# The second layer of six token groups computed with two levels of a seven-product scheme, and four engines put in a fixed order

## The chip, the core and the metric

One core of a Trainium2 chip runs the whole program. It has a matrix engine (PE; PEld is its weight load), a vector engine (DVE), an activation engine (ACT), a GpSimd engine (POOL) and a sync engine (SP) whose queue issues nearly all DMAs. The metric is the device time of one execution in microseconds (us); the time shown is the median of three runs.

## The reference, cut to what matters

The input has 8 batches of 576 tokens, 8 heads of 64, so a model width of 512. Attention with two softmaxes (over the features of q, over the tokens of k) gives x; a Fourier mix and a two-layer network follow.

```python
q_s = softmax(q, axis=-1); k_s = softmax(k, axis=2)          # both written out with max, exp, sum
kv = einsum('bhsd,bhse->bhde', k_s, v)
x = einsum('bhsd,bhde->bhse', q_s, kv)                       # then (B, S, H*D)
u = x + real(fft(fft(x, axis=1), axis=2))
un = (u - mean(u)) / sqrt(var(u) + 1e-06)
out = u + max(un @ w_ch1, 0.0) @ w_ch2                       # w_ch1: 512 x 2048, w_ch2: 2048 x 512
```

## The kernel before, in words

All is in 32-bit floating point. The 4608 tokens are cut into nine groups of 512: one for each batch (group number `g` below 8), and a shared one (`g` equal to `B`) with the tokens that the folding of the Fourier transform treats apart. They are worked on in the order 0 to 6, shared, 7; `order` or `at` counts the place in that order, 0 to 8. Place 0 is computed plainly while the weights are converted and combined. For places 1 to 8 both layers use one level of a scheme that multiplies two 2 x 2 block matrices with seven block products instead of eight. The sums of weight blocks are made once and lie in DRAM (`w1s`, `w2s`).

- **First layer**, `up` (line 945). For each of four `j` there are seven products of 256 x 256 x 256 for each of two hidden pairs, in the order `ORDER` (line 77). `strassen` (line 906) keeps three PSUM banks. Product 1 goes to `ba`, 6 to `bb`, 5 to `bc`; 7 adds onto `bb`, 2 onto `ba`, 4 onto `bb`, 3 onto `bc`. Between them the banks are read: ACT copies `ba` to `s1` (line 921), DVE makes `u2` and `u3` from `bb` (lines 925, 929), `other` adds and ACT applies the relu (lines 968, 969), and POOL makes four sums of hidden blocks (`a_side`, lines 362 to 365).
- **Second layer**, `down` (line 982). Seven products, each 2 halves of tokens times 8 pairs of hidden blocks, so 16 matmuls of 128 x 128 weights with 256 columns (line 995). DVE adds the results to x (line 1020); POOL adds three of the intermediate sums (line 1007).
- **Weights.** The combined weights are fetched again for each place: `load` (line 410) brings chunk `n`, 15 for a place (8 of `w1s`, 7 of `w2s`), into one of four 1 MiB places of `big`. `used` (line 978) releases a chunk after its last matmul and so issues the load of chunk `n + 4`.
- **Work beside it.** While place `order` is computed, the attention of batch `order + 1` runs beside the first layer (`attention`, line 430: keys `k_load`, `k_exp`, `k_turn`, `k_times_v`; queries `q_load`, `q_exp`, `q_turn`, `q_times_kv`; for even batches also a tail item `t`, with `t_turn` and `t_fold`), and the mix (`transform` line 686, `mix_own`, `mix_shared`) and the normalisation of the next group (`norm`, line 816) beside the second.

The order: `merged` (line 93) deals the side steps evenly among the main steps, and the planner of the framework then orders each engine's instructions by priority and its own cost estimates, and sets the semaphores. Each engine runs its instructions in the order it was given. `gate` (line 489) is a tiny DVE instruction that makes a DMA target wait.

Of the kernel before, what the change touches and what calls it, by code (L numbers as in the profile page):

```python
# [40 lines left out]
F32 = mybir.dt.float32  # L41
I32, U32 = mybir.dt.int32, mybir.dt.uint32
ACT = mybir.ActivationFunctionType
ALU = mybir.AluOpType
# [32 lines left out]
ORDER = (1, 6, 5, 7, 2, 4, 3)  # L77

# [45 lines left out]
class _Block:  # L124
    def __init__(self, ctx, tc, q, kT, v, w1, w2, ft, cd, out):
# [42 lines left out]
        self.w2s = d.tile([7, P, NP, HD], F32, tag="w2s", name="w2s", bufs=1)  # L168

# [239 lines left out]

    def load(self, n):  # L410

        g, i = divmod(n, NP + 7)
        if g > B:
            return
        k = n % 4
        w = self.big[:, k * NP * HD:(k + 1) * NP * HD].rearrange("p (a n) -> p a n", n=HD)
        if i < NP:
            self.nc.sync.dma_start(w[:, 0:7, :], self.w1s[i][:])
        else:
            self.nc.sync.dma_start(w, self.w2s[WB_AT[ORDER[i - NP]]])  # L420
        self.stream[n] = w

    def hpairs(self, p, n):

        a = 2 * NF * D + p * 7 * HD if p < NP // 2 else NF * D + (p - NP // 2) * 7 * HD
        return self.big[:, a:a + n * 7 * HD].rearrange("p (a s n) -> p a s n", s=7, n=HD)
# [3 lines left out]
    def attention(self, b, loads=None):  # L430


        items = [("k", b, r) for r in range(NR)]
        tail = [("t", b)] if b % 2 == 0 else []
        own = [("q", b, c, u) for c in range(2) for u in range(2)]

        if b == 1:
            items = []
        items = items + tail + own if b else items[:2] + tail + items[2:] + own
        kinds = {"k": (self.k_load, self.k_exp, self.k_turn, self.k_times_v),  # L440
                 "q": (self.q_load, self.q_exp, self.q_turn, self.q_times_kv),
                 "t": (self.t_load, self.q_exp, self.t_turn, self.t_fold)}
        stage = lambda i: (lambda it: kinds[it[0]][i](it))
        load, *stages = [stage(i) for i in range(4)]
        if loads is None:
            stages.insert(0, load)
        else:
            loads += [lambda it=it: load(it) for it in items]
        steps = pipelined(items, stages)

        steps.insert(len(steps) if b else 8, lambda: self.t_times_kv(b))
        return steps
# [45 lines left out]
    def k_load(self, it):  # L498
        nc, (_, b, r) = self.nc, it
        if b == 0:  # L500
            ks, v = self.at_start[:2]
            self.live[it] = [ks[r], v[:, :, r * P:(r + 1) * P]]
            return
        if b == 1:
            self.live[it] = [self.second_at[0][:, r * S:(r + 1) * S], self.second_at[1][r]]
            return
        if r > 1:
            self.keys_to(b, r, *self.key_places())

    def keys_to(self, b, r, k, v):  # L510
        nc = self.nc
        nc.sync.dma_start(k, self.kT[b, r * P:(r + 1) * P, :])
        cols = slice(r * P, (r + 1) * P)
        nc.sync.dma_start(v[:, 0:4, :], self.v[b, 0:512, cols].rearrange("(c p) n -> p c n", p=P))
        nc.sync.dma_start(v[:, 4, :], self.v[b, S - P:, cols])
        self.live["k", b, r] = [k, v]
# [5 lines left out]
    def keys_from(self, b, t):  # L522


        for r in range(2):
            k, v = self.key_places()
            self.keys_to(b, r, k, v)
            self.gate(t, k[0:1, 0:1])
# [9 lines left out]
    def k_exp(self, it):  # L538
        nc, V = self.nc, self.nc.vector
        k = self.live[it][0]  # L540
        m = self.small.tile([P, 1], F32, tag="km", name="km", bufs=3)
        V.reduce_max(m[:], k, axis=AX.X, negate=True)
        rec = self.small.tile([P, 1], F32, tag="krec", name="krec", bufs=3)
        nc.scalar.activation(k, k, ACT.Exp, bias=m[:, 0:1], accum_out=rec[:, 0:1])
        V.tensor_scalar(out=rec[:], in0=rec[:], scalar1=ATT_EPS, scalar2=None, op0=ALU.add)
        V.reciprocal(rec[:], rec[:])
        self.live[it].append(rec)
# [15 lines left out]
    def k_times_v(self, it):  # L563
# [3 lines left out]
        for c in range(NC):  # L567
            nc.tensor.matmul(pk, lhsT=ks[:, c, :], rhs=v[:, c, :], start=(c == 0), stop=(c == NC - 1))  # L568
        for h in range(2):
# [29 lines left out]
    def q_exp(self, it):  # L599
        nc, V = self.nc, self.nc.vector  # L600
        q = self.live[it][0]
        heads = q.rearrange("p (h d) -> p h d", h=H)
        spread = lambda t: t[:].unsqueeze(2).to_broadcast([P, H, DH])
        m = self.small.tile([P, H], F32, tag="qm", name="qm", bufs=3)
        V.reduce_max(m[:], heads, axis=AX.X, negate=True)  # L605
        for h in range(H):
            nc.scalar.activation(heads[:, h, :], heads[:, h, :], ACT.Exp, bias=m[:, h:h + 1])  # L607
        rec = self.small.tile([P, H], F32, tag="qrec", name="qrec", bufs=4)
# [3 lines left out]
        if it[:2] == ("q", 0) and it[2] == it[3]:  # L612


            self.live[it].append(spread(rec))
            return
# [21 lines left out]
    def t_fold(self, it):  # L638
# [4 lines left out]
        for e, op, i in ((G, ALU.add, 0), (V, ALU.subtract, 2)):  # L643
            e.tensor_tensor(out=T[:, :, i, 1:NT], in0=q[:, :, 1:NT], in1=q[:, :, W - 1:W - NT:-1], op=op)
            e.tensor_tensor(out=T[:, :, 1 + i, 1:NT - 1], in0=q[:, :, Q - 1:Q - NT + 1:-1],
                            in1=q[:, :, Q + 1:Q + NT - 1], op=op)
        n = NT - 1
# [5 lines left out]
    def q_times_kv(self, it):  # L653
# [3 lines left out]
        for r in range(NR):  # L657
            nc.tensor.matmul(px[:, r * P:(r + 1) * P], lhsT=qT[:, r, :], rhs=self.kvr[b % 2][:, r, :], start=True,  # L658
                             stop=True)
        x = self.xpart(b, c, u)  # L660
# [6 lines left out]
    def t_times_kv(self, b):  # L667
# [9 lines left out]
        nc.scalar.copy(self.xshared(b // 2)[part], px[W:])  # L677
        V.scalar_tensor_tensor(out=g[:, 1:HD], in0=g[:, D - 1:HD:-1], scalar=self.sign[:, 0:1], in1=g[:, 1:HD],
# [3 lines left out]
        self.live["g", b] = g  # L682
# [3 lines left out]
    def transform(self, b):  # L686
# [36 lines left out]
        def folded():  # L723
            columns_again()
# [39 lines left out]

        folds = [tokens_folded, columns_folded, by_frequency, folded] if b else [at_first]
# [140 lines left out]
    def strassen(self, product, out, early=lambda *a: None):  # L906
# [30 lines left out]
        for m in ORDER:  # L937
# [4 lines left out]
            steps.append(begin + parts + end)  # L942
        return steps

    def up(self, at, unT):

        nc, V = self.nc, self.nc.vector
        steps = []
        for j in range(NP // 2):
            pairs = (2 * j, 2 * j + 1)  # L950
            hp = lambda i, h=self.hpairs(2 * j, 2): h[:, :, i, :]

            def product(m, bank, first, last, pairs=pairs):
                def run(i):
                    w = self.stream[15 * at + pairs[i]]
# [19 lines left out]
            steps.append([s for m in job for s in m] + [lambda p=p: self.used(15 * at + p) for p in pairs])  # L975
# [6 lines left out]
    def down(self, g, at):  # L982
        nc, V = self.nc, self.nc.vector
        h = [self.hpairs(p, 1)[:, 0] for p in range(NP)]
        last = at == B

        def product(m, bank, first, final):
            n = 15 * at + NP + ORDER.index(m)
# [3 lines left out]
            def run(i, q):  # L992
                w = self.stream[n]
                for p in range(4 * q, 4 * q + 4):
# [36 lines left out]
        return [s for m in steps for s in m]  # L1031
# [22 lines left out]
def kernel(ctx: ExitStack, tc: tile.TileContext, q, kT, v, w1, w2, ft,  # L1054
# [56 lines left out]

    groups = [*range(B - 1), B, B - 1]
    for order, g in enumerate(groups):
        loads = [] if g == 0 else None
        one, two = front(order + 1, loads) if order + 1 < B else (blk.later, [])
        if g == 0:
# [16 lines left out]
            combine[NP:NP] = [lambda i=i: blk.load(15 + i) for i in range(3)]  # L1133
            combine.append(lambda: blk.load(18))
# [26 lines left out]
        jobs, down = blk.up(order, nexts.pop(g)), blk.down(g, order)  # L1161
# [57 lines left out]
```

## Time and profile before

| what | value |
|---|---|
| median of three runs | 1124.38 us (1123.99 to 1129.22) |
| the profiled execution's own time | 1128.05 us |
| its span, first to last instruction | 1126.2 us |
| mean granted TensorE clock | 0.991 |
| PE busy | 1088.4 us (97%) |
| DVE, ACT, POOL busy | 545.4, 403.5, 331.9 us |
| DMA | 193.79 MB, mean 172 GB/s |

A matmul of 32-bit numbers shows as two PE instructions ("passes") in the trace, each with its weight load. A pass's listed duration (379 ns for 256 columns) includes the time in which the next one has already begun, so the cost of a pass is the distance to the next: the chain of waits merges neighbouring passes, and its "us" over its "xcount" is that distance. In the lines of groups the columns are: source line, engine, operation, out<-in, shapes, count, then busy us and mean ns, then the engine's idle time before them with what ended it. In the timeline they are start, duration, engine, line, operation. The page's slices and the stretches ("windows") give busy us of each engine, the granted clock, the DMA engines' mean busy share and GB/s.

### The profile page before, as it was taken

Reading aid. Unit: us, or ns where it says so; the run is one execution under the profiler, and the core shown is the slowest. Engines: PE = TensorE matmul, PEld = TensorE weight load, DVE = VectorE, ACT = ScalarE, POOL = GpSimd, SP = SyncE. Lnnn points to the kernel's source line nnn. Section 1 sums busy time; section 2 is a strip of 40 time slices with the busy share of each in tenths; the row PEclk is TensorE's granted clock in tenths of the full one; section 3 lists DMA queues with packets and bytes.
Section 4 is the critical chain, followed back from the end, with each engine's and each line's share of the span. In section 5 each row is a group of like instructions: output and inputs, shape, how many; then the busy total and the mean of one; then the engine's idle time right before and its main releaser. Section 6 shows DMA issues by size and latency. Waiting matters only on the chain.

```text
span 1126.2 us, 14461 instructions
## 1 busy us (share of the span) xinstructions
PE 1088.4 (97%) x5376; PEld 909.9 (81%) x5376; DVE 545.4 (48%) x1121; ACT 403.5 (36%) x973; POOL 331.9 (29%) x303
## 2 busy tenths in 40 slices
PE   5789989999999999999999999999999999999997
PEld 4644545887888888898889888888889888888886
DVE  6694796368423734375344643583444352103301
ACT  6695434255233513362325332542334152201200
POOL 1065571235013510324024402251034203402320
PEclk8899999999999999999999999999999999999999
DMA  9555786464246534554356435642453444434451
GB/s 305 176 190 188 259 291 220 145 224 166 98 150 211 195 127 145 195 172 171 125 173 221 150 106 190 198 185 108 147 191 150 144 144 144 187 141 157 152 187 56
DMA packets 92581, 193.79 MB, mean 172 GB/s; under 512 B 23120, under 2 KB 59728, under 8 KB 85344
## 3 DMA queue, kind: packets, MB, share of 16 engines
q1 hardware_dynamic: 90712, 191.82, 49.9%
q10 hardware_dynamic: 1800, 1.05, 0.3%
q8 instruction: 43, 0.70, 0.2%
q14 instruction: 26, 0.21, 0.1%
HBM read 168.72 MB, written 28.31 MB: 175 GB/s over the span
## 4 chain that ended last, share of the span: by engine, by line
PE 81%; POOL 3%; issue 2%; ACT 1%; DVE 1%; ACTq 0%; POOLq 0%
PE bb L957 14%; PE bb L995 14%; PE bc L995 10%; PE ba L957 9%; PE bc L957 9%; PE ba L995 9%; PE acc L568 2%; PE acc L658 2%; PE bc L896 2%; PE acc L752 1%; PE acc L776 1%; PE acc L755 1%; PE tr L857 1%; PE tr L554 1%; PE tr L623 1%
## 5 line engine op out<-in xcount | busy, mean ns | idle before, releaser
L957 PE MATMUL bb<-unT,big 128*128 128x256 f32 x768 | 187.4, 381 | 0.2 <-DVE u L925 0.2
L995 PE MATMUL bb<-big 128*128 128x256 f32 x768 | 172.1, 379 | 0.0
L957 PEld LDWEIGHTS bb<-unT,big 128*128 128x128 f32 x768 | 142.8, 190 | 23.9 <-DVE u L925 3.0
L995 PEld LDWEIGHTS bb<-big 128*128 128x128 f32 x768 | 145.4, 190 | 20.3
L362 POOL TENSOR_TENSOR big<-big 128x512 f32<-128x512 f32 (+1 forms) x38 | 46.2, 1216 | 307.6 <-ACT big L969 306.8
L969 ACT ACTIVATE big<-big 128x512 f32<-128x512 f32 x96 | 60.3, 629 | 182.7 <-DVE big L968 182.2
L957 PE MATMUL bc<-unT,big 128*128 128x256 f32 x512 | 125.4, 379 | 0.0
L957 PE MATMUL ba<-unT,big 128*128 128x256 f32 x512 | 123.6, 379 | 0.2 <-ACT unT L861 0.2
L995 PE MATMUL bc<-big 128*128 128x256 f32 x512 | 116.0, 379 | 0.5 <-DVE x L1012 0.5
L995 PE MATMUL ba<-big 128*128 128x256 f32 x512 | 114.8, 379 | 0.0
L929 DVE TENSOR_TENSOR u<-bb,s 128x512 f32<-128x512 f32 x40 | 27.6, 691 | 173.1 <-PE bb L995 116.1
L995 PEld LDWEIGHTS bc<-big 128*128 128x128 f32 x512 | 96.1, 190 | 14.3 <-DVE x L1012 0.9
L995 PEld LDWEIGHTS ba<-big 128*128 128x128 f32 x512 | 95.7, 190 | 12.1
L957 PEld LDWEIGHTS bc<-unT,big 128*128 128x128 f32 x512 | 95.1, 190 | 12.6
L957 PEld LDWEIGHTS ba<-unT,big 128*128 128x128 f32 x512 | 95.1, 190 | 12.2 <-ACT unT L861 0.5
L370 POOL TENSOR_TENSOR unT<-unT 128x512 f32<-128x512 f32 x8 | 14.2, 1772 | 179.8 <-DVE unT L369 179.8
L607 ACT ACTIVATE q<-q,qm 128x64 f32<-128x64 f32 x240 | 61.6, 338 | 6.8 <-DVE qm L605 6.6
L925 DVE TENSOR_TENSOR u<-bb,s 128x512 f32<-128x512 f32 x40 | 27.5, 688 | 71.7 <-PE bb L957 38.7
L968 DVE TENSOR_TENSOR big<-bc,u 128x512 f32<-128x512 f32 x64 | 44.1, 689 | 22.8 <-PE bc L957 21.7
L1007 POOL TENSOR_TENSOR x<-x,u 128x512 f32<-128x512 f32 x14 | 17.7, 1267 | 118.8 <-DVE u L929 99.0
L861 ACT COPY unT<-tr 128x512 f32<-128x512 f32 x36 | 20.7, 585 | 79.9 <-PE tr L857 79.3
L968 DVE TENSOR_TENSOR big<-bb,s 128x512 f32<-128x512 f32 x32 | 22.1, 691 | 56.1 <-PE bb L957 56.1
(254 smaller groups left out, 1640.8 us busy)
## 6 DMA issues: line engine op xcount, KB each, us to landing
big<-w1s SPq DMA_DIRECT2D x64, 896.0 KB
big<-w2s SPq DMA_DIRECT2D x56, 1024.0 KB
big<-in_w_dram SPq DMA_DIRECT2D x21, 512.0 KB
q<-in_q_dram SPq DMA_DIRECT2D x27, 256.0 KB
k<-in_kT_dram SPq DMA_DIRECT2D x24, 288.0 KB
v<-in_v_dram SPq DMA_DIRECT2D x24, 256.0 KB
words<-in_w_dram SPq DMA_DIRECT2D x8, 512.0 KB
mirror<-x SPq DMA_DIRECT2D x14, 256.0 KB
```

What stands on the lines that cost most here:

```text
L362: e1.tensor_tensor(out=to(4), in0=at(2), in1=at(3), op=ALU.add)
L568: nc.tensor.matmul(pk, lhsT=ks[:, c, :], rhs=v[:, c, :], start=(c == 0), stop=(c == NC - 1))
L607: nc.scalar.activation(heads[:, h, :], heads[:, h, :], ACT.Exp, bias=m[:, h:h + 1])
L658: nc.tensor.matmul(px[:, r * P:(r + 1) * P], lhsT=qT[:, r, :], rhs=self.kvr[b % 2][:, r, :], start=True, stop=True)
L861: nc.scalar.copy(unT[:, u:u + 3:2, :, cols], pt[:].rearrange("p (a k) t -> p a k t", a=2))
L896: nc.tensor.matmul(po[:], lhsT=h[:, f, i * P:(i + 1) * P], rhs=self.w2sb[:, f, :], start=(f == 0), stop=(f == NF - 1))
L925: V.tensor_tensor(out=temp("u2"), in0=box["bb"][:], in1=box["s1"][:], op=ALU.add)
L929: V.tensor_tensor(out=temp("u3"), in0=box["bb"][:], in1=box["s1"][:], op=ALU.add)
L957: nc.tensor.matmul(bank()[:, i, :], lhsT=w[:, WA_AT[m], k * P:(k + 1) * P], rhs=unT[:, B_AT[m], k, :], start=first and i == 0 and k == 0, ...
L968: V.tensor_tensor(out=hp(i), in0=bank[:], in1=u[:], op=ALU.add)
L969: nc.scalar.activation(hp(i), hp(i), ACT.Relu)
L995: nc.tensor.matmul(bank()[:, i, :], lhsT=h[p][:, A_AT[m], i * P:(i + 1) * P], rhs=w[:, p, :], start=first and i == 0 and p == 0, stop=p == ...
```

## The change

For the places 2 to 7 the second layer goes one level deeper. Of its seven products the first stays as it is; each of the other six is itself computed with seven products of quarter blocks: 4 matmuls of 128 x 128 weights with 128 columns for each. The six are taken in three units of two, `UNITS`; a unit's two products share the three banks. The weight sums for this are made once, during the second layer of place 1 (`deepen`), and stored to DRAM as `w2d`, from where they come in chunks of four inner products. The sums of hidden blocks are made in each group by DVE and POOL (`a_step`), into places that are free by then. POOL adds all results to x (`into`, `sums`) in place of DVE and POOL.

For the same places the order of the DVE, POOL, PE and ACT instructions is no longer left to the planner: every step has a time in slots (one slot is half a first-layer product), the list is sorted by it, and inside `tc.manual_schedule` the four engines keep that order. SP is not among them. To give each part its own time, steps are split (`k_exp` into `k_max` and `k_sum`, `q_exp` into `q_max`, `q_some` and `q_sum`, and so on). Steps that would end after the second layer move to the start of the next place. In half of the query items of batch 2 and later, the division by the sum moves from q (DVE) to the result (DVE, in place of a copy by ACT). The first-layer chunks are paired (j, j + 4).

```diff
+UNITS = ((2, 4), (7, 6), (5, 3))
+DEEP = [(m, n) for unit in UNITS for n in ORDER for m in unit]
+DOWN_END = 8 + 3 * 2 * len(ORDER)
+PAIRS = [(j + NP // 2, j) for j in range(NP // 2)]
...
+        self.w2d = d.tile([P, len(DEEP), GT], F32, tag="w2d", name="w2d", bufs=1)
...
+    def deep(self, at):
+        return 1 < at < B
...
+    def attention_timed(self, b, end):
+        items = [("k", b, r) for r in range(NR)] + ([("t", b)] if b % 2 == 0 else [])
+        items += [("q", b, c, u) for c in range(2) for u in range(2)]
+        gap, steps = (end - 10) / (len(items) - 1), []
...
+        for i, it in enumerate(items):
+            t = i * gap
+            if it[0] != "k":
+                for h in range(0, H, 2):
+                    put(t + 0.5 + h / 2, self.q_some, it, (h, h + 1))
+            if it[0] != "k":
+                put(t - 6.5, getattr(self, it[0] + "_load"), it)
+            elif it[2] > 1:
+                put(t - 5.5, lambda it=it: self.keys_to(*it[1:], *self.key_places()))
+                put(t - 2.5, lambda it=it: self.values_to(*it[1:], self.live[it][1]))
+            if it[0] == "k":
+                for dt, f in ((0, self.k_max), (2, self.k_sum), (3, self.k_turn), (6, self.k_times_v), (7.7, self.k_scale)):
+                    put(t + dt, f, it)
+            elif it[0] == "q":
+                for dt, f in ((0, self.q_max), (5, self.q_sum), (6.5, self.q_turn), (9, self.q_times_kv), (10, self.q_out)):
+                    put(t + dt, f, it)
+            else:
+                for dt, f in ((0, self.q_max), (5, self.q_sum), (7, self.t_turn), (9, self.t_fold)):
+                    put(t + dt, f, it)
...
-        if it[:2] == ("q", 0) and it[2] == it[3]:
+        if it[0] == "q" and it[1] != 1 and it[2] == it[3]:
...
+    def deepen(self, m, w, t):
...
+        e1.tensor_tensor(out=to(4), in0=at(1), in1=at(0), op=ALU.subtract)
+        e1.tensor_tensor(out=to(1), in0=at(3), in1=at(1), op=ALU.subtract)
+        e2.tensor_tensor(out=to(5), in0=at(3), in1=to(4), op=ALU.subtract)
+        e2.tensor_tensor(out=to(6), in0=at(2), in1=to(5), op=ALU.subtract)
+        for n in (1, 2, 3, 5, 7, 6, 4):
+            i = B_AT[n]
+            to_dram = self.w2d[:, DEEP.index((m, n)), :].rearrange("p (f n) -> p f n", n=P)
+            nc.sync.dma_start(to_dram, to(i) if i in (1, 4, 5, 6) else at(i))
+
+    def deep_down(self, g, at, unT):
...
+        def a_step(m, o):
+            x, y, e, op = {4: (2, 3, V, ALU.add), 5: (4, 0, V, ALU.subtract), 2: (0, 2, V, ALU.subtract),
+                           6: (1, 5, G, ALU.subtract)}[o]
...
+        def into(u, d, m):
+            x = self.xs[g, u][:, :, d * HD:(d + 1) * HD].rearrange("p c (e n) -> p c e n", n=P)
+            G.tensor_tensor(out=x, in0=x, in1=tile(m), op=ALU.add)
...
+        def product(unit, n, i):
...
+            for f in range(4):
+                r = q % 4 * 4 + f
+                nc.tensor.matmul(box[place[n]][:, i, :], lhsT=own(m)(A_AT[n])[:, f, :],
+                                 rhs=w[:, r // 2, r % 2 * P:r % 2 * P + P], start=first and f == 0, stop=f == 3,
+                                 skip_group_check=True)
+            if q % 4 == 3 or q == len(DEEP) - 1:
+                self.used(chunk)
...
+            if n == 1:
+                nc.scalar.copy(temp("s1"), box["ba"][:])
+            if n == 6:
+                plus(temp("u2"), "bb", "s1")
+            if n == 7:
+                plus(temp("u3"), "bb", "s1")
+                plus(out(3), "bc", "u3")
+            if n == 2:
+                nc.scalar.copy(out(0), box["ba"][:])
+            if n == 4:
+                plus(out(2), "bb", "s1")
+            if n == 3:
+                plus(out(1), "bc", "u2")
...
+        for n in range(4):
+            put(2 * n, single, n // 2, n % 2)
+        put(9, into, 0, 0, 1)
+        n = 2 * len(ORDER)
+        for i, unit in enumerate(UNITS):
+            t = 8 + n * i
+            for k, o in enumerate((4, 5, 2, 6)):
+                for j, m in enumerate(unit):
+                    put((0 if i == 0 else t - n + 2) + 3 * k + j * 1.2 + 0.3, a_step, m, o)
+            for k, o in enumerate(ORDER):
+                for j in range(2):
+                    put(t + 2 * k + j, product, unit, o, j)
+                put(t + 2 * k + 1.5, ends, unit, o)
...
+                if at == 1 and m != 1 and (i, q) == (order[0], 0):
+                    self.deepen(m, w, spare if k % 2 else [self.gap(i) for i in range(4)])
...
+        end = 46
+        steps = blk.attention_timed(b, end)
+        dts = (0, 0, 3, 3, 5, 5.5, 7, 11)
...
+        two = [((2, 4, 6, 8, 10)[k], lambda k=k: make()[1][k]()) for k in range(5)]
+        return steps, two + [(13 + 4 * i, s) for i, s in enumerate(mixes)]
...
+        return [(t, lambda i=i: run(i)) for i, t in enumerate((26, 29, 31, 33, 35, 37, 40))]
...
+        if timed:
+            end = 8 * len(ORDER)
+            steps = jobs + one + [(t + end, s) for t, s in down + two + timed_norm(groups[order + 1])]
+            rest = after_all
+            after_all = [(t - end - DOWN_END, s) for t, s in steps if t >= end + DOWN_END]
+            with tc.manual_schedule(engines=engines):
+                for _, s in sorted(rest + [s for s in steps if s[0] < end + DOWN_END], key=lambda s: s[0]):
+                    s()
+            continue
```

## The prediction

> **What bounds the kernel now.** First the page's shares, then its slices, then who made PE wait in the stretch of places 1 to 7.
>
> ```profile
> PE 1088.4 (97%) x5376; PEld 909.9 (81%) x5376; DVE 545.4 (48%) x1121; ACT 403.5 (36%) x973; POOL 331.9 (29%) x303
> ...
> PE   5789989999999999999999999999999999999997
> ```
>
> ```profile
> PE acc L568 <- ACT ks L555: 1.2, 2, 0.6
> ```
>
> PE is the bound: from 300 to 1000 us its waits add up to 1.2 us (second answer, the whole list). So the change gains exactly what it takes off PE, and any wait that it puts on PE counts in full. The chain of waits from 700 to 800 us gives the price of a pass by its distance to the next:
>
> ```profile
> 700.27 1.11 PE acc L568 x10
> ...
> 726.58 0.89 PE acc L658 x8
> ...
> 746.22 6.91 PE ba L995 x32
> ```
>
> A pass of 256 columns costs 6.91/32 = 0.216 us, one of 128 columns with weights of its own 0.89/8 = 0.111 us, a hair over half. The timeline near 24.4 us has 21 such passes in one row, still 111 ns apart, so it is no effect of a short burst. That is where the gain can come from. What can eat it is DVE beside POOL:
>
> ```profile
> 749.36 1.45 POOL L699 TENSOR_TENSOR eo<-x 128x512 f32<-128x512 f32 x1
> 749.60 1.75 DVE L699 TENSOR_TENSOR eo<-x 128x512 f32<-128x512 f32 x1
> ```
>
> ```profile
> L372 DVE TENSOR_TENSOR unT<-unT 128x512 f32<-128x512 f32 x8 | 13.1, 1641 | 0.3
> ...
> L369 DVE TENSOR_TENSOR unT<-unT 128x512 f32<-128x512 f32 x8 | 5.5, 692 | 3.4 <-ACT unT L861 3.4
> ```
>
> The same addition takes DVE 0.69 us alone and 1.6 to 1.75 beside a POOL instruction. In a row DVE's 0.69 us instructions follow each other every 0.60. The stretches of one group and of a full DMA load:
>
> ```profile
> 446.00:566.00 120.00, 119.38 (x634) 105.45 (x633) 63.48 (x127) 44.30 (x113) 34.13 (x29) 1.00 0.50 168
> ```
>
> ```profile
> 185.00:195.00 10.00, 10.00 (x33) 5.07 (x32) 6.03 (x21) 5.90 (x9) 0.00 (x0) 1.00 1.02 342
> ```
>
> A group takes 120 us, in which DVE is busy 63, ACT 44, POOL 34 and the DMA engines half of the time. A full DMA moves 342 GB/s.
>
> **What the Trainium skill says.** *SBUF — State Buffer*, section "SBUF: two separate sides": DVE with two SBUF inputs and POOL take turns on a shared port pair, each holding it for the whole instruction. The trace agrees (1.75 against 0.69 us). *TensorE: Matmul & The Clock Gate*, section "LDWEIGHTS (loading the stationary operand)": a load costs its columns over 1.2, so 107 ns for 128 columns, as much as a 128-column pass; the trace lists 190 ns for a load, but the 111 ns distance shows that loads hide. The same page's table at its head: DVE, ACT and POOL queues are strict FIFO, so what stands behind a waiting instruction waits too. *DMA: Bandwidth & Descriptors*, "Issuing engines are not separate DMA queues": all share 16 engines, so new traffic is added to old.
>
> **Part 1, the passes.** A product of the second layer is 16 matmuls, 32 passes, 6.91 us. Its deep form is 7 x 4 matmuls, 56 passes of 0.111, so 6.23 us. Gain 0.68 us each, six products in six groups: 36 x 0.68 = **24.5 us**. The bounds are narrow: 108 ns a pass (half of 216) gives 31, 112 gives 23.
>
> **Part 2, DVE, POOL and ACT in the second layer.** Added for a group: 18 DVE sums of hidden blocks (0.69), 6 on POOL (1.27); 15 DVE bank reads of half size (0.42, as L791 has from PSUM) for 6 of 0.69; 11 POOL additions (1.27) for 3. DVE +12.4 + 6.3 - 4.1 = 14.6 us, POOL +7.6 + 10.2 = 17.8 us. The division moved out of q saves two of 0.69 to 0.89 and adds two of 0.69: nothing. Of these DVE sums all have two SBUF inputs and take turns with POOL: 12.4 + 21.6 us in a second layer of some 54. So this work fits beside PE on the average and costs nothing there. If that cover were gone, it would be up to 14.6 us a group.
>
> What costs are the deadlines. An inner product lasts 16 passes, 1.78 us, instead of 6.9. `u2` must be out of bank `bb` before product 7, one product after 6 ends: 0.2 (the end of PE's pipeline) + 0.42 + 0.1 leaves 1.0 us of slack for whatever stands ahead in DVE's queue. I follow the queues in the order of the time line, with the durations above, for the places where an earlier entry can be late:
>
> - *Normalisation*, slots 26 to 31. DVE's statistics stand behind `u2` of the second unit, which waits for PE until slot 26. From there: 0.6 for `u2`, four times 0.60 + 0.09 for statistics (2.8), root on ACT 0.3, two small DVE steps 0.3, then ACT's second table load 1.28 and 0.2 and the first normalised tile 0.8, with 0.3 of hand-overs: 6.6 us. PE comes to the transposes of that tile after six inner half-products, 6 x 0.89 = 5.3 us, and everything on PE is queued behind them. Wait **1.3**. The table loads are in the trace:
>
> ```profile
> 790.47 0.30 ACT L830 ACTIVATE std<-mv,eps 128x4 f32<-128x4 f32 x1 [4.18 <-DVE mv L827]
> 790.79 1.28 ACT L837 ACT_TABLE_LOAD   x1
> 792.08 0.20 ACT L837 ACTIVATE root<-std 128x1 f32<-128x1 f32 x1
> ```
>
> - *Query items in the first layer.* `q_turn` follows `q_sum` by 1.5 slots. For the second item of an odd batch, counted from slot 28 on: DVE's bank read for line 968 ends at 0.9, ACT's relu 1.6, its last four exponentials 2.6, the result of the item before (a bank read, which waits for PE) 3.5, sum and reciprocal 4.4, then the multiply, up to 1.28 behind one of the four POOL sums of `a_side`, 6.4. PE gets to the transposes after five slots of 0.864 and 0.89: 5.2. Wait **1.2** (0 to 2). The third item, behind `u3` and line 968 at slot 35.5, needs 3.0 and has 1.7: **1.2**. In even batches the `t` item takes its place, 0.9.
> - *Small ones*: Z blocks whose PSUM tile ACT has not emptied, product 4 behind a mix (seven DVE entries that wait for ACT), `u2` behind a sum that POOL holds up: 0.2 each and a little, together **0.9** (0 to 3).
>
> That is 4.6 us in each of five groups and 1.4 in the sixth (place 7, with no attention and no mix): **24.4 us** of new waits. The range for one group is 1.2 to 6.5. The waits that exist (1.2 us) are too few to give anything back.
>
> **Part 3, `deepen` in place 1.** 12 DVE and 12 POOL sums (8.3 and 15.2 us) lie beside PE's 58 us and cost nothing there. Its 42 DMAs of 256 KB, 11.0 MB, go in 512-byte pieces; such packets take 28 ns in this trace, 291 GB/s over 16 engines, so 37.8 us. With seven 1 MB chunks (20), keys and values (4) and outputs the DMA needs more than the 58 us of that layer, but three chunks are ahead (8 us). SP waits for POOL's last sum with the later loads behind it. I take **3** us of late chunks (0 to 10).
>
> **Part 4, DMA in the deep groups.** 42 x 256 KB + 1 MB replace 7 MB: 4.5 MB more, so 168 becomes about 208 GB/s, share 0.62. A chunk serves 32 passes, 3.56 us, which is 295 GB/s against 342 and with three chunks ahead: hidden. If not, each chunk would add up to its own excess, under 0.5 us. But the stores of a group now fall at the start of the next place (slots 1 and 4), ahead of the key loads of slot 4 on SP's queue; 1.5 MB of them take 6 us, and the third keys have 6 us until DVE needs them. DVE would wait with `u2` behind it. I take 0.7 a group, **3.5** us (0 to 17.5).
>
> **The sum.** 1128.05 (the profiled execution's own time; span 1126.2) - 24.5 + 24.4 + 3 + 3.5 = 1134.5, that is +6.4. The profiled execution lies 3.7 above the median of 1124.38, so on the median: **1130.8 us**. About 0.5% (5.6 us) is what a measurement can tell from no change.
>
> **The rivals.**
> - *Faster: the entries are there in time.* DVE and ACT run ahead in their queues, because earlier waits on PE have let them catch up, and the multiply meets no POOL sum. Then 1.2 us a group are left: -24.5 + 7.2 + 3 = -14.3, **1110**. It decides below 2.6 us of waits a group ((24.5 - 3 - 5.6)/6). For it: DVE is busy only half of the group's time before. Against it: the normalisation's 6.6 us are a chain without slack. Chance 0.28; with `deepen` hidden too, 1107.
> - *Break-even*, waits of 3 to 3.5 a group: **1124**, 0.12.
> - *DMA order decides.* The keys are late by 3.5 in five groups (+14) and place 1 costs 6: **1148**, 0.11. For it: the SP queue is in order. Against it: the share stays near 0.62.
> - *The deep form isn't cheaper*, because weight loads set the pace over hundreds of passes (124 ns a pass would take the gain away): **1155**, 0.04. Against it are the 21 passes.
>
> The forecast itself has 0.45, of which 0.15 lie within 0.5%. Faster 0.28, same 0.27, slower 0.45. The range, 1107 to 1148, reaches over the faster rival and the DMA's.
>
> **What would show it.** Right: the deep passes 111 ns apart; PE's list of waits with transposes (`tr` from `eo`, `tr` from `q`) behind ACT and DVE, 4 to 5 us a group; DVE near 610 to 640 us. Wrong: waits of PE under 2.6 us a group (then it is faster), waits for `big` from DMA (then much slower), or passes over 115 ns.

## The result, and the profile after

The changed kernel takes **1169.1 us** (median of 3 runs, 1167.1 to 1170.8), against 1124.4: ratio 1.038, 95% interval 1.033 to 1.043, slower. The prediction of 1130.8 with its range up to 1148 was too low.

The page of the changed kernel, in the rows that were shown of the kernel before, and the granted clock:

```profile
PE 1076.2 (92%) x6240; PEld 923.0 (79%) x6240; DVE 666.7 (57%) x1295; ACT 409.4 (35%) x997; POOL 476.9 (41%) x399
...
PE   5699899999798899989998999899988999999997
...
PEclk9999999999999999999999999999998999999999
```

PE was busy 1088.4 us of a span of 1126.2; now 1076.2 of 1164.9. So 12.2 us less busy time and **50.9 us more idle time**: together they are the difference of the spans, 38.7. The passes did get cheaper. The chain of waits of the changed kernel between 415 and 440 us (start, us, what):

```profile
420.41 1.79 PE bb L1197 x16
```

That is 0.112 us a pass, 1 ns over the estimate. From 200 to 1010 us, where the waits of PE in the kernel before add up to 4.2 us, those of the changed kernel add up to 52.4. The longest are (us in total, times, longest):

```profile
PE tr L723 <- DVE q L717: 21.7, 10, 3.6
PE tr L980 <- ACT eo L974: 15.6, 6, 7.0
PE bb L1080 <- DVE u L1052: 6.8, 5, 1.4
PE acc L869 <- DVE eo L838: 2.9, 1, 2.9
PE bb L1178 <- DVE big L1091: 2.0, 5, 0.4
```

The first two are the waits that the prediction named, transposes of query items (`q`) and of normalised tiles (`eo`), the former at nearly twice its size. Where they fall is told by the length of each layer, from its first matmul in the trace to that of the next layer (us, sums for places 2 to 6; the other kernels are the experiments below; layers and PE busy are of one profiled execution, which can lie some us from the median in the last column):

| kernel | place 1, 2nd layer | places 2-6, 1st layers | places 2-6, 2nd layers | PE busy | time, us |
|---|---|---|---|---|---|
| before | 60.8 | 311.3 | 289.7 | 1088.4 | 1124.4 |
| after | 70.9 | 350.3 | 283.0 | 1076.2 | 1169.1 |
| planner_up | 73.1 | 353.5 | 287.9 | 1082.1 | 1178.1 |
| temps_once | 62.9 | 350.8 | 281.4 | 1073.4 | 1160.4 |
| turns_late | 73.1 | 348.4 | 282.9 | 1079.3 | 1165.3 |
| combined | 62.8 | 342.1 | 280.1 | 1070.3 | 1151.7 |
| aside_off | 71.2 | 327.2 | 281.4 | 1067.8 | 1140.1 |
| no_fold | 71.3 | 333.3 | 279.7 | 1069.5 | 1147.1 |
| join_late | 62.9 | 330.4 | 287.6 | 1076.7 | 1142.6 |
| late_few | 62.6 | 316.7 | 281.8 | 1066.4 | 1123.6 |

The second layers, which the change rewrites, gain 6.7. The loss is in the **first** layers (+39.0), which hold the same matmuls as before, and in place 1 (+10.1); of the remaining -3.7, place 0 has -3.8. In the five first layers PE is idle for 32.4 us (1.2 before), and DVE is busy for 209.8 us (158.2 before), POOL for 129.8 (100.0 before): the change moved their work there. One wait of the first layer in place 2 shows how. The timeline of the changed kernel (start, us, engine, line; in brackets what it waited for):

```profile
366.36 1.27 POOL L380 TENSOR_TENSOR big<-big 128x512 f32<-128x512 f32 x1
366.85 1.07 DVE L796 SCALAR_TENSOR_TENSOR eo<-eo,sign 128x255 f32<-128x255 f32 x1
367.59 1.45 POOL L381 TENSOR_TENSOR big<-big 128x512 f32<-128x512 f32 x1
367.95 1.25 DVE L798 TENSOR_TENSOR eo<-eo 128x128 f32<-128x128 f32 x1
369.12 1.26 POOL L382 TENSOR_TENSOR big<-big 128x512 f32<-128x512 f32 x1
369.23 1.30 DVE L799 TENSOR_TENSOR eo<-eo 128x128 f32<-128x128 f32 x1
370.45 0.67 DVE L709 TENSOR_REDUCE qrec<-q 128x8 f32<-128x512 f32 x1
371.61 0.69 DVE L717 TENSOR_TENSOR q<-q,qrec 128x512 f32<-128x512 f32 x1
372.35 1.11 PE L723 MATMUL tr<-ident,q 128*128 128x128 f32 x4 [3.56 <-DVE q L717]
```

L796 to L799 are `g_fold`, three instructions on small tiles. Each ends 0.15 to 0.3 us after a POOL sum of `a_side` ends, and lasts 1.07 to 1.30 us. Behind them in DVE's queue stands the sum (L709 to L717) that PE's transposes need. And PE pays twice. The stretches around this wait (from, to; length, then PE, PEld, DVE, ACT, POOL busy; PEclk, DMA share, GB/s):

```profile
368.26:371.67 3.41, 0.54 (x3) 0.13 (x1) 3.27 (x6) 0.00 (x0) 2.04 (x2) 1.00 0.01 3
371.67:375.08 3.41, 2.73 (x9) 2.35 (x10) 1.82 (x3) 2.15 (x8) 0.00 (x0) 0.50 0.10 30
```

In the second stretch the clock is at 0.50, so half of PE's 2.73 us there, 1.4 us, is lost. The Trainium skill, *TensorE: Matmul & The Clock Gate*, section "Part 1: The HAM clock gate", says that an idle window of about 3.4 us halves PE's clock; this wait of 3.56 us agrees, but waits of 2.0 us did the same in other runs (last section).

### The profile page after: what moved, and what is told of

Same layout as the page of the kernel before. It is cut to its first block, busy times and chain, and to the rows that moved or that the text cites. A ratio compares the mean times of both kernels' runs of the same rounds, so it can differ in the third digit from the quotient of the medians.

```text
span 1164.9 us, 16791 instructions
## 1 busy us (share of the span) xinstructions
PE 1076.2 (92%) x6240; PEld 923.0 (79%) x6240; DVE 666.7 (57%) x1295; ACT 409.4 (35%) x997; POOL 476.9 (41%) x399
## 4 chain that ended last, share of the span: by engine, by line
PE 61%; DVE 19%; ACT 4%; issue 3%; POOL 3%; DMA 2%; SPq 0%; DVEq 0%; POOLq 0%; ACTq 0%
PE bb L1080 11%; PE bb L1197 7%; PE ba L1080 7%; PE bc L1080 7%; PE bc L1197 4%; PE ba L1197 4%; PE bb L1178 2%; PE acc L646 2%; PE bc L1273 2%; PE ba L1273 2%; PE bb L1273 2%; PE acc L763 2%; PE bc L1019 1%; DVE st L949 1%; DVE eo L822 1%
## 5 line engine op out<-in xcount | busy, mean ns | idle before, releaser
L379 POOL TENSOR_TENSOR big<-big 128x512 f32<-128x512 f32 (+1 forms) x38 | 46.7, 1230 | 305.3 <-ACT big L1092 304.5
L1080 PEld LDWEIGHTS ba<-unT,big 128*128 128x128 f32 x512 | 94.6, 190 | 11.9 <-ACT unT L984 0.5
L1197 PE MATMUL bb<-big 128*128 128x128 f32 x768 | 95.2, 278 | 1.0 <-DVE u L1204 1.0
L1197 PEld LDWEIGHTS bb<-big 128*128 128x128 f32 x768 | 90.9, 194 | 1.2 <-DVE u L1204 1.2
L1158 POOL TENSOR_TENSOR x<-x,big 128x512 f32<-128x512 f32 x45 | 59.5, 1335 | 58.0 <-ACT big L1183 22.7
L1154 DVE TENSOR_TENSOR big<-big 128x512 f32<-128x512 f32 x84 | 70.0, 863 | 6.0 <-POOL big L382 6.0
L1197 PE MATMUL ba<-big 128*128 128x128 f32 x576 | 71.0, 275 | 0.0
L1052 DVE TENSOR_TENSOR u<-bb,s 128x512 f32<-128x512 f32 x34 | 23.4, 690 | 82.9 <-PE bb L1080 61.3
L1197 PEld LDWEIGHTS ba<-big 128*128 128x128 f32 x576 | 68.4, 192 | 1.2
L1154 POOL TENSOR_TENSOR big<-big 128x512 f32<-128x512 f32 x24 | 39.2, 1651 | 59.6 <-DVE big L1154 59.6
L1048 DVE TENSOR_TENSOR u<-bb,s 128x512 f32<-128x512 f32 x34 | 23.4, 689 | 57.5 <-PE bb L1080 44.1
L382 POOL TENSOR_TENSOR big<-big 128x512 f32<-128x512 f32 x32 | 47.7, 1491 | 2.4
L380 POOL TENSOR_TENSOR big<-big 128x512 f32<-128x512 f32 (+1 forms) x38 | 47.3, 1244 | 2.4
L1197 PE MATMUL bc<-big 128*128 128x128 f32 x384 | 46.8, 275 | 0.0
```

Source lines behind the costliest of these rows:

```text
L379: e1.tensor_tensor(out=to(4), in0=at(2), in1=at(3), op=ALU.add)
L380: e1.tensor_tensor(out=to(2), in0=at(0), in1=at(2), op=ALU.subtract)
L382: e2.tensor_tensor(out=to(6), in0=at(1), in1=to(5), op=ALU.subtract)
L1048: V.tensor_tensor(out=temp("u2"), in0=box["bb"][:], in1=box["s1"][:], op=ALU.add)
L1080: nc.tensor.matmul(bank()[:, i, :], lhsT=w[:, WA_AT[m], k * P:(k + 1) * P], rhs=unT[:, B_AT[m], k, :], start=first and i == 0 and k == 0, ...
L1154: e.tensor_tensor(out=to(o), in0=to(x), in1=to(y), op=op)
```

## Experiments

Theory at first: the order written out by hand makes DVE's entries late, and the planner would do better. Rival: the work that was moved into the first layers is too much beside POOL, in whatever order. Ratios are to the kernel before, with their 95% intervals.

**planner_up.** The steps of the first layer are issued in the same sequence, outside the fixed order.

```diff
-            with tc.manual_schedule(engines=engines):
-                for _, s in sorted(...): s()
+            todo = sorted(...)
+            for t, s in todo:
+                if t < end: s()
+            with tc.manual_schedule(engines=engines):
+                for t, s in todo:
+                    if t >= end: s()
```

> First layer and the attention beside it of places 2 to 7 ordered by the planner again, the second layer still on the time line. Theory 1 (the fixed order of the first layer makes PE wait behind late DVE entries): the first layers of places 2 to 6 fall from 67.5 to 72.6 us back to about 62 to 63, together -37 us, so about 1132. Theory 2 (the added DVE, POOL and DMA work of the second layer spills over, in whatever order): the first layers stay over 66 us, time within 10 us of 1169.

1178.1 us, ratio 1.047 (1.045 to 1.048). The first layers stay at 69.8 to 72.4, and most of PE's waits change their names:

```profile
PE tr L980 <- ACT eo L974: 22.3, 7, 12.2
PE bb L1080 <- DVE u L1052: 15.1, 6, 3.5
```

These are the figures of the rival. The second half of the first theory falls: the planner does no better with these steps. Its first half, that this order by hand makes entries late, isn't settled by this run; late_few below shows it.

**planner_both.** `tc.manual_schedule` is replaced by an empty context, for both layers.

> The same steps in the same list, but the planner orders all engines in both layers of places 2 to 7. Theory 1 (fixed order of the first layer): first layers as in the run above, and the second layers, whose waits on the time line are only 2 to 3 us, change little: 1125 to 1140. Theory 2 (the added work spills over in whatever order): 1165 or more.

1193.3 us, 1.062 (1.059 to 1.065); the second layers rise from 283.0 to 300.6 in sum, in a profiled execution 6 us above the median. The hand-written order is worth up to 3.5 us in each second layer (17.6 over five).

**gfold_late.** `put(t + 2, self.g_fold, b)` becomes `put(t + 5, ...)`.

> One step moved: the three DVE instructions of g_fold go from 2 to 5 slots after the tail's product, behind the sum of the next query item. If g_fold, held up by POOL's four sums on the shared port, makes q_sum late (theory 1): the wait of 3.7 us in places 2, 4 and 6 falls under 1.5 and PE's clock no longer drops after it, 4 to 5 us each, so about 1155. If q_sum is late because DVE waits for the result of the item before (rival): the wait stays over 2.5 us, time 1163 to 1169.

1162.4 us, 1.032 (1.030 to 1.034). The longest wait at line 723 falls from 3.6 to 2.0 us, their sum from 21.7 to 17.0, the first layers by 6.8: right in kind, about half in size. (Places 3 and 5, at 67.5 each, don't change; there `g_fold` has slot 39 instead of 31.)

**deepen_pool.** In `deepen`, `e1, e2 = nc.gpsimd, nc.gpsimd`: all four sums of a product on POOL.

> In place 1 all four weight sums of deepen are made by POOL, none by DVE. If DVE's 6.5 us wait for the store of an earlier sum (a temporary place that is written again) delays the normalisation and so PE (theory 1): PE's wait of 7.2 us at the first transposes falls under 2 us, about 1162. If place 1 is bound by its DMA anyway (rival): the wait of PE moves to a chunk of big, the second layer of place 1 stays near 71 us, time 1166 to 1172.

1178.2 us, 1.045 (1.041 to 1.049). The second layer of place 1 goes up to 78.5, and the wait for the normalised tile there from 7.0 to 11.9. Neither expectation came out. The wait for a store only moved to the other engine: now POOL waits for the stores (`big L1120 <- DMA`, 11.3 us), and DVE for POOL's addition behind that (`x L1298 <- POOL x L1285`, 10.8).

**temps_once.** What DVE waited for in place 1 is in its list of waits, from 255 to 345 us in the changed kernel:

```profile
DVE x L1298 <- PE bc L1273: 11.6, 1, 11.6
DVE big L1120 <- DMA w2d<-big: 11.2, 2, 6.5
```

A set of temporaries is used again for the product after the next, and its stores, in a layer whose DMA share is 0.82, have not left by then. So:

```diff
-                    self.deepen(m, w, spare if k % 2 else [self.gap(i) for i in range(4)])
+                    self.deepen(m, w, spare)
```

> The change kernel with one edit in place 1: each product's four sums go into the hidden block of the product just done, so that no set of temporaries is written twice and DVE and POOL never wait for the stores of an earlier set (11.2 and 15.8 us of such waits in the changed kernel, the normalisation behind them). Theory: these waits in the queue of DVE are why the second layer of place 1 takes 70.9 us instead of 60.8; it falls to about 63 and the time to about 1161. Rival: the stores themselves fill the DMA engines (84% of this layer), chunks and outputs come late whatever DVE does; the layer stays at 69 or more and the time at 1166 to 1171.

1160.4 us, 1.031 (1.028 to 1.033), place 1's second layer at 62.9. `big L1120 <- DMA` is gone from the same list, which now begins:

```profile
DVE x L1298 <- PE bc L1273: 8.4, 1, 8.4
```

PE's wait for the normalised tile there falls from 7.0 to 0.4 us. The theory holds for place 1: not late chunks, but an overwrite that waits for a store, with the normalisation behind it in DVE's queue.

**turns_late.** In `attention_timed` (places 2 to 6), with the items' distance from `(end - 12)` and `t_times_kv` of even batches one slot later:

```diff
-... (6.5, self.q_turn), (9, self.q_times_kv), (10, self.q_out) ... (7, self.t_turn), (9, self.t_fold) ... t + 12, self.t_join
+... (8.5, self.q_turn), (11, self.q_times_kv), (12, self.q_out) ... (8.5, self.t_turn), (10.5, self.t_fold) ... t + 13, self.t_join
```

> The change kernel with one edit in the first layers of places 1 to 6: the transposes of the query items come two slots later on the time line (8.5 after the item's start instead of 6.5, the products with the keys and their outputs two slots later too, the t item 1.5), and the items begin closer together so that the last still ends in time. Theory: PE's waits of 21.7 us for DVE's q_sum, and the fall of the clock behind the longest three (some 5 us), come from the 1.5 slots between sum and transposes, with other entries of DVE's queue ahead of the sum. Waits for q under 5 us, time about 1147. Rival: the lateness is DVE's whole queue, and the same wait comes back two slots later or at line 1080; time 1160 to 1172.

1165.3 us, 1.035 (1.033 to 1.037). The wait for `q` is gone from PE's list, and another is in its place:

```profile
PE tr L980 <- ACT eo L974: 17.0, 7, 6.9
PE bb L1080 <- DVE u L1048: 14.8, 6, 3.9
```

The rival was right: PE now waits for DVE's read of bank `bb`, which stands behind the same late entries.

**norm_fold.** `timed_norm`'s times `(26, 29, 32.5, 34.5, 36.5, 38.5, 41.5)`, and `dts = (0, 0, 4, 3, 5, 5.5, 7, 11)`.

> The change kernel with two edits of the time line: the normalisation's transposes 1.5 slots later, and the transform's column fold on DVE one slot later, behind the read of bank bb for product 4 instead of ahead of it. Theory: PE's wait for the normalised tile (1.7 us in each of five groups) and the one of product 4 for its bank (6.8 us in all at line 1080) are late queue entries and nothing else; they fall to about 2 us each in sum, and the time to about 1156. Rival: the delayed transposes make the next place's first products late, or the fold's delay makes the transform late; time 1164 to 1175.

1168.0 us, 1.038 (1.036 to 1.039). Both waits go (line 980 is left with place 1's 8.0 alone, line 1080's for `u L1052` is gone), and as much comes back behind other entries of DVE: 9.7 us at line 1178, where it was 2.0, and 9.5 at line 1197, where it was 1.0. The 1.1 us that it gains is within the scatter of the changed kernel's own times (1167.1 to 1170.8).

**combined.** The edits of temps_once, turns_late and norm_fold, and `g_fold` three slots later.

> The three edits of this call together, and g_fold three slots later. Theory: the lateness of single entries adds up and nothing else is lost; 1169 less 8 (place 1), 22 (query items), 13 (normalisation and fold) is 1126, about the time of the kernel before. Rival: DVE beside POOL is so full in the first layer (45.6 of 71 us) that a wait removed comes back elsewhere; 1140 or more.

1151.7 us, 1.022 (1.020 to 1.025). That is 17.5 below the changed kernel. The four edits alone give 8.7, 3.9, 1.1 and 6.7, in sum 20.5, so together they give about what they measured one by one, not what the lists of waits promised; the time lies in the rival's range. The trace of this kernel shows the next entry in line, in place 3:

```profile
484.31 0.42 DVE L754 TENSOR_TENSOR F<-T 128x256 f32<-128x256 f32 x1 [5.67 <-POOL T L745]
```

`t_join` on DVE (L754) waits for POOL's part of `t_fold` (L745), which stands behind four sums of `a_side` (478.31 to 483.50); `q_sum` and the read at line 1048 wait behind it.

**aside_off and no_fold**, on the changed kernel itself: `a_side` left out in places 2 to 7; `g_fold`, `columns_folded` and `columns_again` left out for batches 3 and up.

> The change kernel without POOL's four sums of hidden blocks behind each pair of the first layer (a_side), in places 2 to 7; the second layer then reads old values in those blocks. All else, the time line too, stands. Theory: DVE's entries in the first layers are late because POOL's sums hold the port pair that DVE's two-input operations need, and because POOL's own later entries stand behind them; without them the first layers of places 2 to 6 fall from 67 to 73 us to at most 65, and the time by 25 us or more, to about 1140. Rival: POOL has no part in it and the fixed order of the queues is enough to make the entries late; first layers at 66 or more, time 1155 to 1169.

> The change kernel without part of the work that was moved from the second layer into the first: g_fold and the two column folds of the transform (columns_folded and columns_again) are left out for batches 3 and up, so the transform's input is wrong. Theory: this moved work, on DVE and POOL in slots 41 to 57, is what the first layers cannot hide; without it they fall by 3 us or more each and the time by 15 or more, to 1154 or less. Rival: the query items' own entries are late by themselves; the first layers fall by less than 2 us each, and the time stays at 1160 or more.

aside_off: 1140.1 us, 1.013 (1.010 to 1.016). no_fold: 1147.1 us, 1.019 (1.016 to 1.021). The first layers, 350.3 in sum, fall by 23.1 and by 17.0, out of the 39.0 that they lost. PE's waits without `a_side`:

```profile
PE tr L723 <- DVE q L717: 11.5, 10, 1.6
...
PE bb L1080 <- DVE u L1052: 1.1, 5, 0.3
```

Both theories' times came out (aside_off's first layers at 64.4 to 66.9, for at most 65 expected; no_fold's fall by 2.1 to 5.2 each, for 3 or more): taking away POOL's sums or the moved folds takes away some half of the loss each. Both left out together wasn't run, so how far these halves overlap isn't shown. POOL's sums were in the kernel before too; what is new is what meets them. The waits for `q` halve without `a_side` and don't vanish.

**late_all.** On combined: `t_join` at `t + 17`, `t_times_kv` two slots later; `dts = (0, 0, 4, 3, 8, 8.5, 10, 13)`, the matmuls of the transform and the mixes two slots later; in `a_step`'s time `+ (k == 1 and i > 0) * 2.5`.

> The combined kernel with the four waits that its trace still shows taken away on the time line: t_join four slots later (DVE stood 5.7 us behind POOL in it, PE 4.0 for line 1048), the transform's by_frequency and columns_again and its matmuls two to three slots later, so that the read of bank bb comes first (2.2 us at the start of each second layer), and the second block sum of a unit 2.5 slots later, behind the read for product 4 (1.5 us). Theory: each wait is a single late entry; 1152 less 2 x 4, 5 x 2.2 and 5 x 1.5 is 1125. Rival: the waits move on again, as they did when the transposes alone were put later; 1140 or more.

1146.7 us, 1.017 (1.013 to 1.021). The first layers fall to 323.2 (62.4 in places 3 and 5), but the second ones rise to 301.0. There PE waits 11.9 us at line 1197 for DVE's bank reads and 8.0 for ACT's copy of the first product (line 1183), which in the timeline stands behind the exponentials of a key, those behind a DVE entry, and that behind the later fold. Here the waits moved on, as the rival had it, and the time lies in its range.

**join_late, late_few, late_few2.** join_late is combined with `t_join` at `t + 17` and `t_times_kv` two slots later. late_few moves more single entries and leaves the transform's matmuls where they were:

```diff
-(8.5, self.q_turn), (11, self.q_times_kv), (12, self.q_out)
+(8.5, self.q_turn), (11.8, self.q_times_kv), (12.7, self.q_out)
-dts = (0, 0, 4, 3, 5, 5.5, 7, 11)
+dts = (0.8, 0.8, 4, 3, 7.6, 5.5, 9, 11)
-put(t - 5.5, lambda it=it: self.keys_to
+put(t - 6.2, lambda it=it: self.keys_to
-... + 3 * k + j * 1.2 + 0.3, a_step, m, o)
+... + 3 * k + (k == 1 and i > 0) * 2.5 + j * 1.2 + 0.3, a_step, m, o)
```

late_few2 is late_few without the last of these.

> The combined kernel with one edit: t_join four slots later (and the product that needs it two). In the combined kernel DVE's part of t_join waited 5.7 us for POOL, which had four sums of a_side in front of its own part; PE then stood 4.0 us at line 1080 for DVE's next bank read, in places 3 and 5. Theory: this one entry is all that still keeps those two first layers at 70.3 us; they fall to about 63 and the time from 1152 to about 1137. Rival: with t_join later, the product behind it or g_fold is late; 1145 or more.

> The join_late kernel with four more moves of single entries: the transform's by_frequency on DVE 2.6 slots later and columns_again 2, behind the read of bank bb that the second layer's first product waits for (2.2 us in each of five places in the combined kernel), the second block sum of a unit 2.5 slots later (1.5 us in five places), the query items' products 0.8 slot later (1.6 us in three places), the key loads 0.7 slot earlier, ahead of the stores. Theory: 1137 less 11, 7, 5 is about 1114 to 1120, faster than the kernel before. Rival: each move puts other entries in the way, and 1130 or more remains.

> The late_few kernel with the block sums of a unit at their old slots. Theory: 7 us slower than late_few (1.5 us in five places for line 1197 behind DVE's block sums). Rival: the later block sums make POOL's own late for the next unit, and this one is the faster of the two.

join_late: 1142.6 us, 1.013 (1.011 to 1.015); places 3 and 5 at 64.6, about as expected, but the time not (1137): the second layers are 7.5 longer than in combined, largely because the clock falls to half for 3.41 us at their start in places 3 to 6, and once more in place 6, at 1.7 us each. late_few2: 1126.2, 1.000 (0.999 to 1.001). **late_few: 1123.6 us, 0.998 (0.997 to 0.999)**, 45.5 below the changed kernel and, by a quarter of a percent, below the kernel before (1126.0 when measured beside it); expected were 1114 to 1120. The later block sums are worth 2.5 us, not 7. The page and the longest of PE's waits in late_few:

```profile
PE 1066.4 (95%) x6240; PEld 917.6 (82%) x6240; DVE 664.6 (59%) x1295; ACT 408.6 (36%) x997; POOL 478.7 (43%) x399
```

```profile
PE acc L646 <- ACT ks L633: 10.2, 9, 4.3
PE acc L763 <- ACT qT L730: 8.5, 4, 4.4
...
PE bb L1197 <- ACT big L1183: 3.7, 4, 1.2
PE bb L1197 <- DVE u L1204: 3.6, 6, 1.0
PE acc L869 <- DVE eo L838: 2.9, 1, 2.9
PE tr L980 <- ACT eo L974: 2.3, 7, 0.4
```

DVE and POOL do as much as in the changed kernel (664.6 and 478.7 us), and the first layers hold the same work, yet they are back at 316.7. So there is room for the work, and the rival of the opening, too much of it in whatever order, falls: the order of the entries decides.

## Why the prediction was wrong, point by point

**Part 1, the passes: right.** 0.112 us a pass, so 56 of them take 6.27 and the gain is 36 x 0.64 = 23 us for the 24.5 on record. In late_few, where little else is disturbed, PE's busy time is 22.0 below that of the kernel before; some 4 us of that are not passes but the clock, which in the kernel before was at 0.50 in two stretches of place 0 (17.6 to 24.4 and 34.7 to 41.5 us).

**Part 2, the new waits: right in kind, wrong in size, and this step failed.** On record were 24.4 us. The term that failed is the query items in the first layer: 11.4 us on record for places 2 to 6, where PE was then idle for 32.4 us in these layers and they grew by 39.0. In the second layers the forecast holds: PE was idle there for 8.8 us, with 11.0 on record.
- The normalisation was put at 1.3 a group; the changed kernel has 1.7 (15.6 in all at line 980 from 200 us on, less 7.0 in place 1, over five). This term holds.
- The query items were put at 2.4 (2.1 in even batches). Their own transposes wait for 21.7 us in five groups, 4.3 each, the longest 3.6. The term asked when each item's own chain would be done and let one multiply meet a POOL sum. It left out `g_fold`, which the time line puts ahead of `q_sum`: three DVE entries, all three held up by POOL. gfold_late took 6.8 us off the first layers by moving that alone.
- The small ones were put at 0.9 a group. The places named for them show no wait in places 2 to 6; 6.8 us at line 1080 and 2.0 at line 1178 stand at the end of the first layer instead, 1.8 a group. The former go when the transform's fold is moved (norm_fold), so they are entries behind it.
- "So this work fits beside PE on the average and costs nothing there" was reckoned for the second layer. The first layer got no such reckoning, although the diff moves `g_fold` and the transform's fold to slots 31 to 57, all but the last in the first layer's 56, from a layer where a product of 6.9 us hid them to one where a bank read has one product, 8 passes of 0.216 or 1.73 us, to be in time. no_fold prices it: 17.0 us off the first layers.
- DVE was busy for 666.7 us, outside the 610 to 640 named as a sign, because instructions that POOL holds up count as busy; without `a_side` it is 620.7. It isn't the loss by itself: late_few has 664.6.
- A price for the clock was missing. The changed kernel's PE is busy 9.8 us longer than late_few's with the same 6240 passes. From 200 us to the end of its work PE had six stretches with the clock at 0.50 (from 276.1, 317.1, 371.7, 624.3, 873.4 and 945.1 us; four of 3.41 us, two of twice that) and was busy in them for 22.1 us; half of that, 11.0, is lost. late_few has one such stretch, 2.85 us busy, so 1.4 lost. The difference is 9.6 us: the clock is nearly all of the 9.8.

**Part 3, `deepen` in place 1: wrong mechanism, and at the upper end of its range.** 10.1 us for 3 (0 to 10). The sums "lie beside PE's 58 us and cost nothing there", and late chunks were to be the cost. temps_once shows the other: the sums wait for stores of temporaries used twice, the normalisation waits behind them, and with one set for each product 8.0 of the 10.1 go.

**Part 4, the order of loads: too high here.** PE's waits for keys come to 1.5 us from 200 us on in the changed kernel, for 3.5 on record. In turns_late and combined it rose to 4.3 and 4.5, so it is there when the rest is tight; in late_few, with the loads ahead of the stores, it is 1.2.

**The rivals.** "The entries are there in time" was given 0.28 and had an argument against its cause in the trace of before: DVE beside POOL, 1.75 us for 0.69. The prediction used that for one instruction of a chain, not for every entry ahead of it. What decided was none of the rivals, but the main case with its losses at twice the size: a gain of 22 us, against 51 us more idle time and 10 us of slower passes, where 31 us in all were on record.

**What stays open.** Of the 23 us, late_few keeps 2.4 (1123.6 against 1126.0). Against the kernel before it still has 5.4 us more in the five first layers and 3.6 in both layers of place 1, and in its second layers PE waits 1.1 to 1.7 us each, mostly at line 1197 for bank reads and the copy at line 1183. Whether these can go too wasn't tried. Nor was a run with the one-level second layer on the same time line, which would price the moved folds without the deep form.

## What to carry to other kernels

Before splitting work into pieces with closer deadlines, follow the queue that must meet them in the stage that receives the moved steps, not only in the one that is rewritten, and price every entry ahead of the deadline at what it takes beside the other engine's instructions (here up to 1.40 us for 0.29). A removed wait is gained only when the next entry of the queue is early too: the later transposes and the later normalisation took 22 and some 16 us off the list of waits and 4 and 1 off the time, so read the list again after each edit. A temporary that a store still reads holds up its next writer, and with it all that stands behind in the queue.

## What the hardware showed that was not expected

Whether the clock falls isn't told by the length of the wait alone. In the traces the clock changes only at the edges of steps of 3.41 us. In join_late a wait of 2.01 us lay whole in one step and left PE busy for 1.40 us of it, and in the next step the clock was at 0.50. In temps_once a wait of 3.55 us lay across two steps, which kept 1.55 and 1.73 us, and the clock stayed at 1.00 (first join_late, then temps_once; columns as above):

```profile
510.52:513.93 3.41, 1.40 (x7) 1.24 (x7) 3.21 (x9) 1.23 (x2) 0.09 (x1) 1.00 0.97 320
513.93:517.35 3.42, 3.42 (x9) 2.70 (x9) 3.35 (x5) 0.00 (x0) 3.34 (x3) 0.50 0.71 295
```

```profile
613.22:616.63 3.41, 1.55 (x8) 1.02 (x6) 3.34 (x4) 0.45 (x1) 3.06 (x3) 1.00 0.24 92
616.63:620.05 3.42, 1.73 (x10) 1.58 (x11) 2.73 (x6) 1.15 (x4) 0.00 (x0) 1.00 0.02 4
```

From 190 to 1060 us of the sixteen traces there are some 4000 such steps at full clock. After 76 of them the clock fell: PE had been busy for at most 0.44 of 75 of these steps (0.50 of the other), and for at least 0.44 of every step after which it did not fall. So a step needn't be idle throughout, as the "idle window" of the cited section suggests, and the same wait can cost up to 1.7 us more or nothing, by where it lies in the steps.

A DVE addition of two 128x128 tiles took 0.29 us alone (501.35 us in combined) and 1.25 to 1.40 beside a POOL sum, over four times as long:

```profile
501.35 0.29 DVE L798 TENSOR_TENSOR eo<-eo 128x128 f32<-128x128 f32 x1
501.68 1.40 DVE L799 TENSOR_TENSOR eo<-eo 128x128 f32<-128x128 f32 x1
```

One of two 128x512 tiles went from 0.69 to 1.75 us beside a POOL instruction in the kernel before, so small instructions suffered most.
